# Two edits at the start of a tuned state-space kernel: the source of the warm-up matmuls, and the size of the transposing loads of B

## The chip, the cores and the metric

The kernel runs on one core of one Trainium2 chip. The metric is the device time of one execution in microseconds (us), lower is better. A time is the span of the profile plus about 1.8 us (the profiled run of the kernel before took 247.9 us with a span of 246.1). All times compared here are of runs at a granted TensorE clock of 0.997 to 1.0 of full speed. Each group of experiments below ran on another chip.

## The reference, cut to what matters

The output is a gated mix of two branches over x (2048 tokens of 1024 features, bf16): a diagonal complex state-space model, and a branch that adds a gated MLP to the 8 best-scored tokens.

```python
x = A_x
g = sigmoid((x * gate_w).sum(-1, keepdims=True))
# a: state-space model
Lam_bar = exp(dt * Lam)                              # complex, diagonal
B_bar = ((Lam_bar - 1.0) / Lam)[:, None] * (B_re + 1j * B_im)
Bu = einsum("bld,pd->blp", x + 0j, B_bar)            # needs B_re and B_im transposed
h = Lam_bar * h + Bu[:, t, :]                        # for every t
a = 2.0 * einsum("blp,dp->bld", hseq, C_re + 1j * C_im).real + x * Dskip
# b: x + (silu(x_sel @ w_gate) * (x_sel @ w_up)) @ w_down, for the 8 tokens of highest x @ w_r
return g * a + (1 - g) * b
```

What matters here is the product with B. B_re and B_im are 1024 x 1024 matrices that come to the chip transposed, in eight chunks of 128 rows each (c = 0 to 7); the matmuls use chunk after chunk, re before im.

## The kernel before

The loads stand on the queue of SyncE, in this order (cut):

```python
def load_B(pl, c0, c1):                               # pl 0: re, 1: im; rows c0*128 to c1*128
    nc.sync.dma_start_transpose(BT[pl][:, :, c0 * P:c1 * P], Bsrc[pl][c0 * P:c1 * P, :])

load_B(0, 0, 1)
...
load_xT(1)
load_B(1, 0, 1)
for c0, c1 in ((1, 2), (2, 3), (3, 4), (4, 6), (6, 8)):
    for pl in range(2):
        load_B(pl, c0, c1)
load_X(1)                                             # second block of x: two transposing loads
for pl in range(2):
    load_C(pl, 0)
...
load_X(2)                                             # third block
load_C(0, 512)
load_X(3)                                             # last block
load_C(1, 512)
```

TensorE is kept busy with matmuls on a tile of zeros until the first tokens are there:

```python
wt0 = small.tile([P, LC], BF16, name="wt0", tag="wt")
nc.vector.memset(wt0[:], 0.0)
...
def warm(n):
    for _ in range(n):
        nc.tensor.matmul(wps[:], lhsT=wt0[:, 0:P], rhs=wt0[:], start=True, stop=True)

warm(14)
```

Then come the products with B, eight matmuls of 512 columns for the re part of a chunk and eight for the im part (the first chunk apart).

```python
def s1u(m, ct, pl, k0, k1):                           # block m, chunk ct, re or im
    ...
    for dc in range(KD):
        nc.tensor.matmul(o, lhsT=BT[pl][:, dc, ct * P:(ct + 1) * P], rhs=X[m][:, dc, k0 * LC:k1 * LC], ...)

def gate_rows():
    zr = ps_m.tile([P, 2 * LC], F32, name="zr", tag="m")
    for dc in range(KD):
        for m in range(4):                            # the last block too
            nc.tensor.matmul(zr[32 * m:32 * m + 32, :], lhsT=rg[:, dc, :], rhs=X[m][:, dc, :], ...)
```

Of the kernel before, what the change touches and what calls it, by code (L numbers as in the profile page):

```python
# [11 lines left out]
BF16 = mybir.dt.bfloat16  # L12
# [4 lines left out]
P = 128  # L17
LC = 256
# [6 lines left out]
def kernel(  # L25
# [19 lines left out]
    nc = tc.nc  # L45
# [3 lines left out]
    NCT = NP_ // P  # L49
# [16 lines left out]
    small = ctx.enter_context(tc.tile_pool(name="small", bufs=1))  # L66
# [12 lines left out]
    def load_B(pl, c0, c1):  # L79
        nc.sync.dma_start_transpose(BT[pl][:, :, c0 * P:c1 * P], Bsrc[pl][c0 * P:c1 * P, :])  # L80
# [18 lines left out]
    new_X(0)  # L99
    load_xT(1)  # L100
    load_B(1, 0, 1)
    for c0, c1 in ((1, 2), (2, 3), (3, 4), (4, 6), (6, 8)):
        for pl in range(2):
            load_B(pl, c0, c1)
    load_X(1)
# [19 lines left out]

    stpool = ctx.enter_context(tc.tile_pool(name="stpool", bufs=2))

    wt0 = small.tile([P, LC], BF16, name="wt0", tag="wt")
    nc.vector.memset(wt0[:], 0.0)
    Dbc = const.tile([P, D], BF16, name="Dbc")  # L130
    halfpi = small.tile([P, 1], F32, name="halfpi")
    nc.vector.memset(halfpi[:], math.pi / 2)
# [15 lines left out]
    wps = ps_m.tile([P, LC], F32, name="wps", tag="m")  # L148

    def warm(n):  # L150
        for _ in range(n):
            nc.tensor.matmul(wps[:], lhsT=wt0[:, 0:P], rhs=wt0[:], start=True, stop=True)

    warm(14)
    vec = small.tile([P, 3, NCT], F32, name="vec")
    for tl in range(BPC):
        xq = ps_s2.tile([P, KD, P], BF16, name="xq", tag="zps")
# [2 lines left out]
        for h, copy in enumerate((nc.vector.tensor_copy, nc.scalar.copy)):  # L160
            hs = slice(h * KD // 2, (h + 1) * KD // 2)
            copy(out=X[0][:, hs, tl * P:(tl + 1) * P], in_=xq[:, hs, :])
    warm(2)
    va_ps = ps_m.tile([P, 3, NCT], BF16, name="va_ps", tag="m")
    for i in range(3):
# [230 lines left out]

    tab_neg(0)
    warm(1)
    s1u(0, 0, 0, 0, 1)
    warm(2)  # L400
# [547 lines left out]
```

## Time and profile before

| | kernel before |
|---|---|
| three timed runs | 247.28, 247.49, 247.5 us |
| the run that was profiled | 247.9 us (span 246.1) |
| TensorE busy | 240.6 of 246.1 us |
| the wait for B_im, chunk 4 | 0.89 us |
| the tail: start of VectorE's last instruction to the end of the span | 3.18 us |

In the lines of the profile PE is TensorE, PEld its loading of weights, DVE VectorE, ACT ScalarE, POOL GpSimd and SPq the queue of SyncE; L485 is line 485 of the kernel. First, the page's list of DMA queues (queue, kind: packets, MB, share of 16 engines):

```profile
q8 instruction: 11, 0.18, 0.3%
q14 instruction: 6, 0.05, 0.1%
```

The engines' own instructions come in by DMA too. 17 packets and 0.3% look like nothing, but each of the eleven is 16 KB in one packet.

### The profile page before, as it was taken

What the parts mean: (1) busy time and instruction counts of PE and PEld (TensorE: products, weight loads), DVE (VectorE), ACT (ScalarE), POOL (GpSimd) and SP (SyncE); (2) the same over time, 40 slices, a digit from 0 to 9 for tenths busy, and PEclk for the clock granted to TensorE, in tenths of its full rate; (3) what the DMA queues carried; (4) which work ended last, traced back from release to release, by engine and by line L of the source; (5) the groups of instructions that cost most, each with busy time, mean ns of one, the idle gap of its engine ahead of it and who ended that gap; (6) DMA issues with size and microseconds to landing.
All of it is one profiled execution on the core that took longest, in us unless ns stands there. A gap on an engine that the chain in (4) does not pass through costs nothing.

```text
span 246.1 us, 3533 instructions
## 1 busy us (share of the span) xinstructions
PE 240.6 (98%) x1381; PEld 112.2 (46%) x1381; DVE 226.2 (92%) x230; ACT 119.3 (48%) x206; POOL 26.8 (11%) x47
## 2 busy tenths in 40 slices
PE   8998999999999999999999999999999999999994
PEld 5443444444444444444444444444444444446453
DVE  1799999999999999999999999999999999999932
ACT  3699973333462572223355462235267445456421
POOL 4000000000000301620002040100100211110210
PEclk9999999999999999999999999999999999999999
DMA  7899999999760450666257979778599999962052
GB/s 195 194 149 226 230 244 273 202 239 284 236 181 0 106 153 0 134 125 224 77 188 218 351 226 338 237 224 314 184 390 286 363 306 296 89 142 37 3 133 82
DMA packets 65313, 48.48 MB, mean 197 GB/s; under 512 B 50560, under 2 KB 52224, under 8 KB 65296
## 3 DMA queue, kind: packets, MB, share of 16 engines
q1 hardware_dynamic: 59968, 37.20, 58.1%
q0 software_dynamic: 3264, 7.38, 14.3%
q10 hardware_dynamic: 2064, 3.68, 4.1%
q8 instruction: 11, 0.18, 0.3%
q14 instruction: 6, 0.05, 0.1%
HBM read 27.55 MB, written 8.40 MB: 146 GB/s over the span
## 4 chain that ended last, share of the span: by engine, by line
PE 89%; SPq 7%; DMA 2%; issue 0%; DVE 0%
PE zps L767 42%; PE vps L271 39%; SPq L80 6%; PE zps L783 3%; PE pgu L659 3%; DMA BT<-in_A_B_im_dram 2%; PE y L671 1%; SPq L92 1%; PE zr L485 1%; DVE ot L788 0%; SPq L77 0%; PE xselT_ps L572 0%; PE zs_ps L588 0%; PE zt L492 0%; PE fl_ps L535 0%
## 5 line engine op out<-in xcount | busy, mean ns | idle before, releaser
L271 PE MATMUL vps<-X,BT 128*128 128x512 bf16 (+1 forms) x520 | 112.6, 376 | 1.2 <-DMA BT<-in_A_B_im_dram 0.9
L767 PE MATMUL zps<-CT,H 128*128 128x512 bf16 x480 | 105.0, 379 | 0.0
L271 PEld LDWEIGHTS <-BT 128*128 128x128 bf16 x520 | 50.1, 98 | 61.7 <-DMA BT<-in_A_B_im_dram 1.7
L767 PEld LDWEIGHTS <-H 128*128 128x128 bf16 x480 | 46.5, 98 | 56.6 <-issue 1.3
L278 ACT CAST V<-vps 128x512 bf16<-128x512 f32 x64 | 34.3, 588 | 58.6 <-PE vps L271 58.6
L308 DVE TENSOR_TENSOR_SCAN U<-d,U 128x2048 bf16<-128x2048 f32 (+2 forms) x22 | 62.0, 2860 | 0.6
L772 ACT ACTIVATE ot<-zps,gcol 128x512 bf16<-128x512 f32 x30 | 20.6, 686 | 46.3 <-PE zps L767 46.3
L741 ACT CAST zps<-xd 128x512 f32<-128x512 bf16 (+1 forms) x29 | 16.6, 576 | 3.6 <-ACT xt L728 3.3
L297 DVE TENSOR_TENSOR U<-V,T2tab 128x4096 bf16<-128x4096 bf16 (+2 forms) x11 | 16.6, 1511 | 0.7 <-ACT V L278 0.2
L298 DVE TENSOR_TENSOR V<-V,nTi 128x4096 bf16<-128x4096 bf16 (+2 forms) x11 | 16.7, 1516 | 0.5
L299 DVE TENSOR_TENSOR U<-U,V 128x4096 bf16<-128x4096 bf16 (+2 forms) x11 | 16.7, 1516 | 0.4
L793 POOL DMA_DIRECT2D out_dram<-ot x14 | 12.9, 923 | 32.5 <-ACT ot L772 30.4
L333 DVE TENSOR_TENSOR U<-U,S2tab 128x4096 bf16<-128x4096 bf16 x7 | 16.0, 2292 | 0.2
L335 DVE TENSOR_TENSOR H<-H,U 128x4096 bf16<-128x4096 bf16 x7 | 16.0, 2292 | 0.2
L728 ACT ACTIVATE xt<-xt,omgcol 128x1024 bf16<-128x1024 bf16 x14 | 16.0, 1144 | 0.0
L331 DVE TENSOR_TENSOR H<-U,Ctab 128x4096 bf16<-128x4096 bf16 x7 | 16.0, 2284 | 0.0
L705 POOL DMA_DIRECT2D xt<-in_A_x_dram x12 | 7.1, 594 | 80.9 <-DMA out_dram<-xt 42.9
L366 DVE TENSOR_TENSOR_SCAN U<-D,U 128x1024 bf16<-128x1024 f32 x4 | 8.9, 2279 | 0.1
L723 DVE TENSOR_TENSOR xd<-xt,Dbc 128x1024 bf16<-128x1024 bf16 x14 | 9.0, 683 | 0.0
L659 PE MATMUL pgu<-wgu,xsel 128*32 128x448 bf16 x128 | 7.2, 355 | 0.0
L783 PE MATMUL zps<-CT,H 128*128 128x256 bf16 (+1 forms) x48 | 7.1, 308 | 0.0
L718 POOL DMA_DIRECT2D out_dram<-xt x2 | 1.5, 752 | 49.2 <-DVE xt L717 49.2
(152 smaller groups left out, 127.6 us busy)
## 6 DMA issues: line engine op xcount, KB each, us to landing
wgu<-in_B_w_gate_dram SPq DMA_DIRECT2D x16, 448.0 KB, 3.5
wgu<-in_B_w_up_dram SPq DMA_DIRECT2D x16, 448.0 KB, 6.1
out_dram<-ot POOLq DMA_DIRECT2D x14, 256.0 KB, 6.0
wdb<-in_B_w_down_dram SPq DMA_DIRECT2D x7, 512.0 KB, 10.6
xt<-in_A_x_dram POOLq DMA_DIRECT2D x12, 256.0 KB, 4.3
out_dram<-xt ACTq DMA_DIRECT2D x12, 256.0 KB, 5.2
wd<-in_B_w_down_dram SPq DMA_DIRECT2D x5, 512.0 KB, 7.8
xt<-in_A_x_dram SPq DMA_DIRECT2D x4, 256.0 KB, 4.1
```

The costliest lines, as they stand in the source:

```text
L271: nc.tensor.matmul(o, lhsT=BT[pl][:, dc, ct * P:(ct + 1) * P], rhs=X[m][:, dc, k0 * LC:k1 * LC], start=(dc == 0), stop=(dc == KD - 1))
L278: nc.scalar.copy(out=V[k][:, :, ct, :], in_=vp[m, ct][:, :, kk, :])
L297: nc.vector.tensor_tensor(out=u, in0=v, in1=T2tab[:, :, c0:c1, :], op=ALU.mult)
L298: nc.vector.tensor_tensor(out=v, in0=v, in1=bc(nTi, c0, c1), op=ALU.mult)
L299: nc.vector.tensor_tensor(out=u, in0=u, in1=V[k][:, ::-1, c0:c1, :], op=ALU.add)
L308: nc.vector.tensor_tensor_scan(out=fl, data0=d0[:, c0:c1, :].rearrange("p c t -> p (c t)"), data1=fl, initial=0.0, op0=ALU.mult, op1=ALU.add)
L331: nc.vector.tensor_tensor(out=h, in0=g, in1=bc(Ctab, c0, c1), op=ALU.mult)
L333: nc.vector.tensor_tensor(out=g, in0=g, in1=S2tab[:, :, c0:c1, :], op=ALU.mult)
L335: nc.vector.tensor_tensor(out=h, in0=h, in1=G[k][:, ::-1, c0:c1, :], op=ALU.add)
L741: nc.scalar.copy(out=z[:], in_=xd[b][:, d_:d_ + w])
L767: nc.tensor.matmul(zps[:], lhsT=H[k][:, pl, ct, tl * P:(tl + 1) * P], rhs=CT[pl][:, ct, dsl], start=(fresh and ct == 0 and pl == 0), stop= ...
L772: nc.scalar.activation(out=ots[b][:, dsl], in_=zps[:], func=ACT.Copy, scale=gcol[:, b:b + 1])
```

## The change

The intent: let the warm-up begin without waiting for a memset on VectorE, and let TensorE have chunk 4 of B_im without waiting for chunk 5, which came in the same 256-row load.

```diff
-    for c0, c1 in ((1, 2), (2, 3), (3, 4), (4, 6), (6, 8)):
+    for c0, c1 in ((c, c + 1) for c in range(1, NCT)):
         for pl in range(2):
             load_B(pl, c0, c1)
...
-    wt0 = small.tile([P, LC], BF16, name="wt0", tag="wt")
-    nc.vector.memset(wt0[:], 0.0)
+    wt0 = nc.const_aps.tensor(1.0, [P, LC], BF16)
...
-            nc.tensor.matmul(wps[:], lhsT=wt0[:, 0:P], rhs=wt0[:], start=True, stop=True)
-    warm(14)
+            nc.tensor.matmul(wps[:], lhsT=wt0[:, 0:P], rhs=wt0, start=True, stop=True)
+    warm(16)
```

It adds four DMA instructions and two matmuls, and takes one memset away.

## The prediction

> **What bounds the kernel now.** I read the page first (busy shares, slices, the chain that ended last), then the waits of the TensorE, then the timeline of the first 30 us on the queue of SyncE, and last the timelines of TensorE, ScalarE and VectorE for the slack behind the start.
>
> The page, shares of the span:
> ```profile
> span 246.1 us, 3533 instructions
> PE 240.6 (98%) x1381; PEld 112.2 (46%) x1381; DVE 226.2 (92%) x230; ACT 119.3 (48%) x206; POOL 26.8 (11%) x47
> ```
> PE is busy for 240.6 of 246.1 us, so all that any change of waits can give is in the other 5.5 us, and 2 to 3 us of those are the tail after the last matmul. The view of waits, limited to PE and to the first 40 us, has all the idle time there is:
> ```profile
> PE wps L152 <- DVE halfpi L132: 1.1, 1, 1.1
> PE vps L271 <- DMA BT<-in_A_B_im_dram: 0.9, 2, 0.7
> PE vps L271 <- DMA X<-in_A_x_dram: 0.2, 1, 0.2
> ```
> The reader is to see that the kernel waits for B in just two places, and that the larger is 0.7 us. (The 1.1 us at the start is the time before the first warm-up matmul.) In the chain that ended last, the same wait is the hinge between the loads and the 219 us of unbroken matmuls; the columns are start, length and what ran:
> ```profile
> 14.68 3.56 SPq L80
> 18.24 0.04 issue
> 18.29 5.27 DMA BT<-in_A_B_im_dram
> 23.56 0.05 issue
> 23.61 36.43 PE vps L271 x168
> ```
> So one load of B_im, issued at 18.29, lands at 23.56 and releases PE at 23.61. The timeline says which. On the queue of SyncE, in order of time:
> ```profile
> 11.97 1.31 SPq L80 DMA_TRANSPOSE BT<-in_A_B_re_dram  x1
> 13.33 1.31 SPq L80 DMA_TRANSPOSE BT<-in_A_B_im_dram  x1
> 14.68 3.56 SPq L80 DMA_TRANSPOSE BT<-in_A_B_re_dram  x1
> 18.29 2.42 SPq L80 DMA_TRANSPOSE BT<-in_A_B_im_dram  x1
> 20.75 2.18 SPq L80 DMA_TRANSPOSE BT<-in_A_B_re_dram  x1
> 22.98 2.42 SPq L80 DMA_TRANSPOSE BT<-in_A_B_im_dram  x1
> 25.44 4.40 SPq L92 DMA_TRANSPOSE X<-in_A_x_dram  x2
> ```
> The first two are the last 128-row loads (c=3); the next four are the 256-row loads (c=4..5, then c=6..7, re and im in turn). The one that lands late is B_im rows 4..5: PE wants only its half 4, but gets it when both are there. The size of the loss: the first matmul of re c=4 starts at 20.99 (timeline of PE in short windows), eight matmuls at 36.43/168 = 0.2168 us are 1.73 us, so im c=4 could start at 22.72 and starts at 23.61: 0.89 us lost. (The view of waits says 0.7 as it counts from the modelled end of the matmul before.) Re c=4 itself cost nothing: the matmuls before it start at 20.12, 20.34, 20.55, 20.77, and the next slot is 20.99.
>
> **What the Trainium skill says.** "TensorE: Matmul & The Clock Gate", Part 1 (the HAM clock gate): the array starts at 1.2 GHz and goes to 2.4 after about 3.4 us of activity, in a window that runs free, so that the point varies; cold matmuls start N/1.2 GHz apart. The trace agrees in kind: 14 warm-up matmuls of 256 columns fill 1.07 to 4.13, which is 13 at 256/1.2 = 0.213 us and one short one, so the clock changed near 3.85, some 2.8 us after the first. The same part gives 215.7 ns between warm matmuls of 512 columns; here it is 216.8. "DMA: Bandwidth & Descriptors", Rules for kernel authors, advises 1 MiB or more per DMA and to merge small ones, which speaks against the cut into 256 KB pieces; the same page, Latency and other measured facts, has 261 GB/s for a DMA transpose with a non-contiguous middle dimension. In the trace the 128-row loads went out at 256 KiB per 1.35 us, 194 GB/s; the 256-row ones at 512 KiB per 2.2 to 2.4 us, 218 to 238 GB/s, the first of them at 147. So larger is somewhat faster per byte here too, and no run has yet shown 128-row loads in that place.
>
> **The change part by part.**
> (1) The memset of the warm-up tile (0.17 us on VectorE, from 0.84) goes, and the warm-up reads a constant that the preamble has already written (GpSimd, 0.31 to 0.41). The warm-up waited for VectorE until 1.07. The other engines start at 0.74 to 0.75, so I take PE's start as about 0.80: 0.27 us earlier. Two more matmuls are 2 x 0.213 = 0.43 us if cold, 2 x 0.11 = 0.22 if warm. The last warm-up starts at 0.80 + 15 x 0.213 = 4.0 if all are cold, and leaves PE at about 4.1 to 4.2. Before, the transposes of x began at 4.11 when x0r had landed. So they move by 0 to +0.1 us. Behind them stand three waits for transfers: PE waits at 5.93 for the first B_re (0.24 us on the weight loader), at 7.44 for X (0.24) and at 8.65 for the first B_im (0.18). None of those transfers moves, so a shift of 0.1 ends there. Worth on the path: 0.0.
> (2) Four 256-row loads become eight of 128 rows in the order re 4, im 4, re 5, im 5, re 6 and so on. Issued from 14.68 at 1.35 us each: re 4 at 14.68, im 4 at 16.03, re 5 at 17.4, im 5 at 18.7, im 7 at 24.1 to 25.4. The view of B's tile has 3.4/4.7/5.3 us as least, median and most from issue to landing. With 4.7: im 4 lands at 20.7, wanted at 22.72; re 5 at 22.1, wanted at 20.99 + 16 x 0.2168 = 24.46; im 5 at 23.4, wanted at 26.2. If the odd 0.95 us that the first 256-row issue took above the second-longest kind (3.56 against 2.60 for the X load at 2.57) strikes again, im 4 goes out at 17.0 and lands at 21.7: still 1.0 us early. So the wait at 23.61 goes whole: -0.89 us.
> (3) What comes after. SyncE ends the B loads at 14.68 + 8 x 1.35 = 25.5 against 25.40 before, or 26.4 with the odd stall. X of the second block then lands by 32.4 to 33.6 (second issue plus 5.0, the median of X), and PE wants it at 23.61 - 0.89 + 56 x 0.2168 = 34.86. No wait.
> (4) Does the gain reach the end? ScalarE must empty PSUM: it waited for PE by 0.18, 0.72, 0.49 and 1.43 us in its next evictions, and the one that did not wait, c=5 (29.11 to 30.18), frees the buffer that PE wants for c=7 at 32.28, or 31.39 after. VectorE is 92% busy and moves less than PE: its one wait there is 0.24 us at 36.52, so it gains at most that. Then PE's lead over its inputs shrinks by 0.65 us or more, at most 0.89. The nearest places, VectorE's end against PE's use:
> ```profile
> 73.04 2.29 DVE L335 TENSOR_TENSOR H<-H,U 128x4096 bf16<-128x4096 bf16 x1
> 204.75 2.29 DVE L335 TENSOR_TENSOR H<-H,U 128x4096 bf16<-128x4096 bf16 x1
> 231.50 0.69 DVE L380 TENSOR_TENSOR H<-H,U 128x1024 bf16<-128x1024 bf16 x1
> 235.80 7.11 PE L783 MATMUL zps<-CT,H 128*128 128x512 bf16 x48
> ```
> H of chunk 1 is done at 75.3 and used at 65.50 + 64 x 0.217 = 79.4 (4.1 us free); chunk 6 at 207.0, used near 211.8 (4.8); the first half of the last one at about 232.2, used at 235.80 (3.6). The update rows land at 237.4 and are added by 238.7, where the last add for which they are needed stands at 241.92. All over 0.89. So the sum is 0.0 - 0.89 + 0.0 = -0.89 us, carried by PE to the end: 247.49 - 0.89 = 246.60 us, -0.36%.
>
> **The rivals.**
> (a) The 128-row loads are slower and the wait only moves. For it: per byte they went out 10 to 20% slower than the larger ones, and the skill's advice. Against: im 4 has 1 to 2 us to spare. If it holds, im 4 lands at 22.72 or later, or X of the second block becomes the wait, and the gain is 0 to 0.5: 247.0 to 247.5.
> (b) VectorE takes PE's place as the bound. For it: 92% busy, without idle time of note from 14 to 234 us. Against: the slack of 3.6 us and more above. If it held, nothing of the gain would be left: 247.4.
> (c) The clock. The warm-up ends about where it did, but its two ends move in the free-running window. If the clock came a window later, the matmuls from 5.93 to 10.6 (16 of 256 columns and 8 of 512, 8192 columns, 3.5 us warm) would run cold, and with the waits between them I put 1 to 2 us on it: 247.6 to 248.6. Against: activity begins earlier and has no new gap. If it came earlier, nothing is gained, as x0r and B set the pace there.
> (d) All is hidden or the start gains too: an earlier first matmul brings 0.2 us more, 246.4. Against: three waits for transfers behind it.
>
> **Range and chances.** I give the sum 70%, (a) 15%, (c) 5%, the rest to (b) and (d). The three timed runs before span 0.22 us, which I take as noise of 0.15 to either side, and the sum's own doubt is 0.1 or 0.2. So 246.6, with 246.2 to 247.1 for 8 in 10. A change of 2% is 4.9 us; the idle time of PE before 23.61 is less than that in all. Faster by over 2%: 0.005; slower by over 2%: 0.01, for a clock that stays low or a load that stalls; within 2%: 0.985.
>
> **What would show it.** Right: PE's waits list no wait for B_im over 0.2 us, and the matmuls run unbroken from about 10.6; the eight B issues after c=3 last about 1.3 us each, the first perhaps 2.3; the chain's long run of matmuls begins at about 10.6 and its end is near 242.1; the span is about 245.2. The first warm-up starts near 0.80 and the transposes of x still near 4.1 to 4.2. Wrong: a wait for B or X on PE at 21 to 35 us (rival a), PE waiting for H or zps (b), 0.2 us spacing of 256-column matmuls after 5.9 (c), or a later start of B's first loads on SyncE.

## More of the kernel before

The end. VectorE's last instruction in its timeline, and SyncE's wait on line 943, where the body of the kernel is closed, in the view of waits of its queue (us in total, times, longest):

```profile
242.95 0.48 DVE L788 SCALAR_TENSOR_TENSOR ot<-zps,gcol,xt 128x256 bf16<-128x256 f32 x1 [0.21 <-PE zps L783]
```

```profile
SPq L943 <- DMA out_dram<-ot: 0.8, 2, 0.5
```

The span ends at 246.14, so 3.18 us pass after the last arithmetic begins (the tail; from unrounded times); they hold the last store and the closing waits of SyncE.

Second, TensorE's timeline near 60 us (start, length, engine, line, operation, tiles, shapes, count), where the gate reads the last block of x:

```profile
59.97 1.91 PE L485 MATMUL zr<-X,rg 128*32 128x512 bf16 x32
```

## The result, and the profile after

| | before | after |
|---|---|---|
| timed runs, us | 247.19, 247.28, 247.49, 247.5, 247.58, 247.58 | 247.46, 247.55, 247.55, 247.76, 248.01, 249.09 |
| median, us | 247.5 | 247.66 |
| profiled run, us (span) | 247.9 (246.1) | 247.46 (245.7) |

The ratio is 1.0019, with a 95% interval of 0.9995 to 1.0042: the same time within 2%. This ratio is the mean time of one kernel's fast runs over that of the other's. In the experiments below the ratios leave out the first run of each kernel (of the kernel tested, the profiled one), so they are not quite the ratios of the means given beside them. The predicted 246.6 did not come, nor any time in the range of 246.2 to 247.1.

The page, and the view of waits of TensorE in the first 40 us:

```profile
span 245.7 us, 3541 instructions
PE 241.1 (98%) x1383; PEld 112.7 (46%) x1383; DVE 225.8 (92%) x229; ACT 119.2 (49%) x206; POOL 26.9 (11%) x47
```
```profile
PE wps L151 <- PEq L931: 0.8, 1, 0.8
```

So the wait for B_im is gone, and so is the one for X. The timeline on SyncE's queue shows why (start, length of the issue, line, tile, count):

```profile
14.68 2.38 SPq L80 DMA_TRANSPOSE BT<-in_A_B_re_dram  x1
17.10 1.31 SPq L80 DMA_TRANSPOSE BT<-in_A_B_im_dram  x1
18.45 1.31 SPq L80 DMA_TRANSPOSE BT<-in_A_B_re_dram  x1
...
26.56 4.73 SPq L92 DMA_TRANSPOSE X<-in_A_x_dram  x2
...
52.49 4.13 SPq L92 DMA_TRANSPOSE X<-in_A_x_dram  x2
```

Chunk 4 of B_im went out at 17.10 and landed at 20.90, where the prediction had 20.7 to 21.7, and TensorE wanted it at about 22.6. The chain that ended last (start, length, what ran) now leaves the loads before 9 us:

```profile
8.49 1.90 PE vps L270 x8
...
10.52 48.45 PE vps L270 x224
58.98 2.22 PE zr L484 x32
61.19 3.56 PE vps L270 x16
```

From 10.52 to 58.98 TensorE does not stop. But the gate takes 2.22 us in this chain against 1.84 before (1.91 in the timeline above). The timeline of the weight loads has the reason:

```profile
59.29 1.41 PEld L484 LDWEIGHTS <-rg 128*32 128x32 bf16 x29 [0.29 <-DMA X<-in_A_x_dram]
```

The last block of x, issued at 52.49 to 56.62, landed at 59.25; before it had landed at 55.45. And the end, in the same two views as before:

```profile
242.26 0.48 DVE L787 SCALAR_TENSOR_TENSOR ot<-zps,gcol,xt 128x256 bf16<-128x256 f32 x1 [0.21 <-PE zps L782]
```
```profile
SPq L942 <- DMA out_dram<-ot: 1.1, 1, 1.1
```

VectorE's last instruction begins 0.69 us earlier than before (242.26 against 242.95), but the span ends only 0.45 us earlier (245.69 against 246.14): the tail is 3.42 us instead of 3.18.

The two traces balance as follows. The unbroken run of matmuls began 0.16 us earlier (the first of c=1 at 10.46 instead of 10.62), from there to the gate it took 0.90 less (the wait for chunk 4), the gate 0.38 more, the tail 0.24 more: -0.44, against -0.45 between the two spans. So in this pair of traces the predicted 0.89 us are there, and about two thirds of them were given back in places where the prediction had nothing. But the pair of traces says faster by 0.45 us and the timed runs say slower by 0.16 at the median. The kernel before, then, must usually run without most of the loss that its trace showed. That was to be tested.

### The profile page after: what moved, and what is told of

Read it like the earlier page. It is cut to its first block, busy times and chain, and to the rows that moved or that the text cites. A ratio compares the mean times of both kernels' runs of the same rounds, so it can differ in the third digit from the quotient of the medians.

```text
span 245.7 us, 3541 instructions
## 1 busy us (share of the span) xinstructions
PE 241.1 (98%) x1383; PEld 112.7 (46%) x1383; DVE 225.8 (92%) x229; ACT 119.2 (49%) x206; POOL 26.9 (11%) x47
## 4 chain that ended last, share of the span: by engine, by line
PE 95%; SPq 2%; DMA 1%; DVE 0%; issue 0%
PE vps L270 45%; PE zps L766 42%; PE zps L782 3%; PE pgu L658 3%; DMA BT<-in_A_B_im_dram 1%; PE y L670 1%; SPq L92 1%; PE zr L484 1%; SPq L80 1%; DVE ot L787 0%; SPq L77 0%; PE xselT_ps L571 0%; PE zs_ps L587 0%; PE zt L491 0%; PE vb_ps L435 0%
```

## The experiments

Theories at the start. (i) The wait is a draw: it differs from run to run, the trace before came from a long run, and its mean is well under 0.89. (ii) It is there in every run, and the gain is given back later, at the gate and in the tail. (iii) A delay at chunk 4 is hidden behind some slack, so that taking it away changes nothing. (iv) The new warm-up costs what the loads gain.

Means and medians are of six runs of the kernel, and of eleven of the kernel before in the same rounds. The mean and median of the kernel before were 247.88 and 247.8 in the first group (four kernels), 247.65 and 247.45 in the second (four), 248.34 and 248.12 in the third (four) and 248.39 and 248.27 in the fourth (three).

### First group: the same again, and each part alone

**The kernel before, unchanged.** No edit.

> The kernel before, unchanged, as a control. Theory 1 (the gain at the c=4 wait is real and is given back later, at the gate matmuls, where the profile after shows 0.3 us of waiting for X): its trace again loses 0.8 to 0.9 us at c=4 and nothing at the gate. Theory 2 (the profile of before was an odd draw, it was taken in a run of 247.9 us where the others have 247.2 to 247.6, and the usual wait at c=4 is smaller): the trace loses under 0.5 us at c=4 and its run is 247.2 to 247.6. Time 247.4 for both, ratio 1.000 within 0.001.

Measured: mean 247.77, median 247.57, ratio 0.9987 (0.996 to 1.0014), six runs from 247.27 to 248.76. Its trace is of the 248.76 run. The waits of TensorE, and the queue of SyncE:

```profile
PE vps L271 <- DMA BT<-in_A_B_im_dram: 1.4, 2, 1.0
...
PE vps L271 <- DMA BT<-in_A_B_re_dram: 0.5, 1, 0.5
```
```profile
14.57 4.23 SPq L80 DMA_TRANSPOSE BT<-in_A_B_re_dram  x1
18.84 2.56 SPq L80 DMA_TRANSPOSE BT<-in_A_B_im_dram  x1
```

The same code, another size: the first 256-row issue took 4.23 us, not 3.56, and chunk 4 of B_im landed at 24.41, not 23.56. Now TensorE waits for chunk 4 of B_re too, 1.83 us in all where the trace before lost 0.90, which fits neither of the two sizes expected. The wait is no constant, which is the first half of theory (i). The six runs are also a measure of the noise: the same kernel differs from itself by 0.11 us on the mean, and by 0.32 in the runs of the ratio.

**The kernel after, unchanged.** No edit.

> The changed kernel, unchanged, as a control of its spread: six runs had 247.46 to 249.09, against 0.4 us of spread before. Theory 1: the trace has no wait at c=4 and one of 0.3 us or more on X at the gate matmuls, and the slow runs are those where X comes later still. Theory 2: no wait at the gate in most runs, 247.4. Theory 3 (the warm-up change costs something, for example granted clock, as some of its runs list 0.999): a clock of 0.999 with the slower runs. Time 247.5 to 247.8.

Measured: mean 247.73, median 247.76, ratio 0.9995 (0.9968 to 1.0023). No wait at chunk 4 in its trace; chunk 4 of B_im landed at 20.67. The last block of x landed at 58.02, and here the gate did not wait: what it lost in the first trace is a draw as well. The tail was 3.43, again a quarter of a microsecond longer than before.

**The loads alone**, with the old warm-up:

```diff
-    for c0, c1 in ((1, 2), (2, 3), (3, 4), (4, 6), (6, 8)):
+    for c0, c1 in ((c, c + 1) for c in range(1, NCT)):
```

> Only the eight 128-row loads, with the old warm-up. Theory 1: no wait at c=4, a wait for X at the gate of 0.3 us or more, net 247.2 to 247.7. Theory 2: 247.3, as there is little to win. Theory 3: 246.6 to 246.9, since what costs is left out.

Measured: mean 247.67, median 247.72, ratio 0.9994 (0.9968 to 1.0021). Chunk 4 landed at 20.18; no wait there and, against what theory (ii) expected, none at the gate; tail 3.44.

**The warm-up alone**, with the old loads:

```diff
-    wt0 = small.tile([P, LC], BF16, name="wt0", tag="wt")
-    nc.vector.memset(wt0[:], 0.0)
+    wt0 = nc.const_aps.tensor(1.0, [P, LC], BF16)
...
-    warm(14)
+    warm(16)
```

> Only the warm-up change, with the 256-row loads. Theory 1 and theory 2: as before within 0.1 us (247.4), the c=4 wait as in the control. Theory 3: 247.8 or more, and the spread of the changed kernel comes with it.

Measured: mean 247.58, median 247.57, ratio 0.999 (0.9962 to 1.0018), tail 3.18. In its trace the 256-row loads are the old ones, and there is no wait at chunk 4:

```profile
14.81 3.13 SPq L80 DMA_TRANSPOSE BT<-in_A_B_re_dram  x1
```

The issue took 3.13 us, chunks 4 and 5 of B_im landed at 22.57, and TensorE wanted them at about 22.8 (48 + 8 matmuls after 10.70). So a 256-row load can be in time. Neither part moves the time outside the interval, and theory (iv) has nothing for it. The long tail goes with the loads, not with the warm-up.

### Second group: what the wait is worth, and what a microsecond of it is worth

**No wait by other data.** In the kernel before, chunks 4 to 7 of the first block use chunks 0 to 3 of B, which have long landed. The result is wrong on purpose (though the comparison's tolerance let it pass).

```diff
         for dc in range(KD):
-            nc.tensor.matmul(o, lhsT=BT[pl][:, dc, ct * P:(ct + 1) * P], ...)
+            cb = ct - 4 if m == 0 and ct >= 4 else ct
+            nc.tensor.matmul(o, lhsT=BT[pl][:, dc, cb * P:(cb + 1) * P], ...)
```

> The kernel before, but in the first block column chunks 4 to 7 of B are replaced by chunks 0 to 3, which landed long ago, so no wait for B can arise after c=3 (wrong result on purpose). All loads stay as they are. It measures what the c=4 wait is worth in the timed runs. Theory 1 (0.89 us in every run): 0.8 to 0.9 us under the kernel before. Theory 2 (the wait differs from run to run, the first profile caught a long one): 0.3 to 0.6 us under the mean of before, and the slow tail of before (248.5 and more) is gone. Theory 4 (something else than PE's waits sets the end, so that time on PE is not worth time at the end): under 0.1 us.

Measured: mean 247.38, median 247.42, ratio 0.9992 (0.9966 to 1.0018), six runs from 247.20 to 247.54. Against the kernel before in the same rounds (246.89 to 248.97) the mean falls by 0.26 us and the median by 0.03; what vanishes are the long runs. In its own trace the loads of chunk 4 landed at 22.44, so that this run would have lost nothing had it waited. This sizes the wait: about a quarter of a microsecond on the mean, next to nothing in the median run. The interval, some 0.6 us to either side, is wider than that, and the unchanged kernel differed from itself by as much, so 0.26 is a reading and not a proof. That six runs have no long one, where 3 of 11 are over 248, can also be chance. And it is one chip: the kernel before was slower on two others (medians of 248.1 and 248.3), where this was not run.

**One more load ahead of chunk 4, kernel before.** It goes into a part of the C tile that is filled later.

```diff
             load_B(pl, c0, c1)
+        if c1 == 4:
+            nc.sync.dma_start_transpose(CT[1][:, :, 512:640], Bsrc[1][0:128, :])
```

> The kernel before with one more 128-row transposing load (1.35 us on the queue, into a part of C that is loaded again later) ahead of the loads of c=4. If the c=4 wait is on the path in a usual run, the whole 1.35 us shows at the end: 1.2 to 1.4 us over before (theories 1 and 2). If a usual run has slack there of s us, 1.35 - s. Theory 4: nothing shows.

Measured: mean 248.81, median 248.72, ratio 1.0052 (1.0022 to 1.0082): 1.16 us more on the mean, 1.27 on the median, for an issue of 1.31 us and a gap of 0.04. All six runs are over 248.2. Its trace:

```profile
PE vps L273 <- DMA BT<-in_A_B_im_dram: 0.5, 1, 0.5
```

Chunk 4 of B_im landed at 23.96. Theory (iii) falls: a delay ahead of chunk 4 comes out at the end nearly whole. It also says that the loads have close to no slack in the kernel before: most of its runs stand just at the edge of waiting.

**The same load in the kernel after.** The same edit.

> The changed kernel with the same extra load. If im 4 has the slack of 1 to 2 us that the prediction worked out, PE waits at c=4 by 0 to 0.3 us only, but X of the last block comes 1.35 us later and the gate matmuls wait 1 to 1.7 us in theory 1 (time +1 us or more), 0.3 to 1 us in theory 2. If the 128-row loads leave no slack at c=4: +1.2 us with the wait at c=4.

Measured: mean 248.14, median 248.09, ratio 1.0022 (0.9996 to 1.0049), 0.67 us under the other kernel with the extra load. The single-chunk loads do give the slack that the prediction claimed: nothing waits at chunk 4. What waits is the second block of x, which landed at 35.43, and not the last block at the gate, as was expected:

```profile
35.52 24.33 PE L272 MATMUL vps<-X,BT 128*128 128x512 bf16 x110 [0.56 <-PE vps L272]
```

(The view names a matmul as the releaser; the landing at 35.43 and the start at 35.52 say that it was the transfer.) The next input in the queue is late in turn: the prediction's rival (a), with the load doubled to bring it out.

**The last block of x ahead of C, kernel after.**

```diff
     load_X(2)
-    load_C(0, 512)
     load_X(3)
+    load_C(0, 512)
     load_C(1, 512)
```

> The changed kernel with X of the last block loaded ahead of the second half of C, so that the gate matmuls at 59 us cannot wait for it. Theory 1 (gain given back at the gate): 0.3 us or more under the changed kernel (247.4 or less against 247.7), smaller spread. Theory 2 (the wait at the gate is an odd draw as well): within 0.2 us of the changed kernel. The trace has no wait for X at the gate under either.

Measured: mean 247.36, median 247.31, ratio 0.9986 (0.996 to 1.0013), 0.3 us under the kernel before on the mean. The last block's first half landed at 53.7, and the gate does not wait. It fits a loss at the gate in some runs of the kernel after, but the interval takes in no change.

### Third group: the tail, the gate, a better order, and what draws the wait

**Four tiny loads more, kernel after.** If the tail depends on how many DMAs there are, four 128-byte loads will change it.

```diff
+    scr = small.tile([1, 4, 64], BF16, name="scr")
...
     def zero_last():
+        for i in range(4):
+            nc.sync.dma_start(scr[:, i, :], x2d[i:i + 1, 0:64])
```

> The changed kernel with four tiny loads (128 bytes each, unused) added on SyncE's queue in the middle. The traces so far have 3.14 to 3.20 us from the start of the last VectorE instruction to the end of the span in the kernels with the 256-row loads, and 3.44 to 3.46 in those with eight 128-row loads. Theory 5 (the closing waits: eight semaphores are dealt in turn to the DMAs and waited for one by one in a fixed order at the end, some 60 ns each; four more loads move the last store's semaphore from the fifth place to the first, so that the rest is waited for after it): with eight more DMAs than before the place is the old one, and the tail is 3.15 to 3.20 again, time 0.25 us under the changed kernel. If the tail belongs to the 128-row loads in another way, it stays at 3.45.

Measured: mean 248.11, median 248.26, ratio 0.9985 (0.9953 to 1.0018). The tail went back to 3.18 us, and SyncE's last wait reads `DMA out_dram<-ot: 0.8, 2, 0.5`, as in the kernel before. The records of SyncE after its last store show the mechanism. They are a row of equal waits, each of 28 ns, and all are done about 60 ns apart except where a store is still under way:

| kernel | the wait for the last store ends ... us before the end | waits still to come | tail, us |
|---|---|---|---|
| before | 1.092 | 3 | 3.18 |
| after | 1.339 | 7 | 3.42 |
| after, unchanged again | 1.339 | 7 | 3.43 |
| after, four tiny loads more | 1.094 | 3 | 3.18 |
| before with two more loads (below) | 0.973 | 1 | 3.06 |

The kernel ends by waiting once for each of a fixed row of semaphores. The records of DMAs name eight of them in turn, so four more or fewer DMAs anywhere in the kernel move the last store from one place in the row to another. Before, the last store stood late in the row; after, it is first, all others are checked behind it, and 4 x 0.06 us come on top. With eight more DMAs it is back where it was. The two kernels with one extra load, traced before this was looked for, fit as well: their last store stands one place later in the row than without it, and their tails are 3.12 and 3.37.

What undid the gain in this trace was the gate:

```profile
60.54 1.90 PE L485 MATMUL zr<-X,rg 128*32 128x512 bf16 x29 [1.07 <-DMA X<-in_A_x_dram]
```

The last block of x landed at 60.50, and from the product before the gate to the one after it TensorE lost 1.46 us, the largest loss so far (the view counts 1.07 of it as idle). The tiny loads come far behind, so up to here this is the kernel after: another draw of the same race.

**The kernel after, a third time.** No edit.

> The changed kernel a third time, beside the two above on the same chip: 247.5 to 247.8 on average, no wait at c=4, X of the second block landing at 33.3 to 34.6 against the 34.7 at which PE wants it, tail 3.45.

Measured: mean 248.18, median 248.14, ratio 0.9994 (0.9963 to 1.0025). No wait at chunk 4; the last block of x landed at 59.60, and the gate lost 0.15 us. Tail 3.43.

**The fetch of instructions, moved.** In every trace but that of this experiment one packet of 16,384 bytes comes on the instruction queue at 14.7 to 17.1 us. While it is under way some of the 256-byte packets of the transposing queue, 18 ns at the median, take far longer, the longest of each trace 1.27 to 2.49 us, and in all 17 traces the issue that runs at that time is a long one:

```text
trace                    packet at   took   longest packet of B   the long issue   chunk 4 of B_im landed
before                   16.72       0.95   1.43                  3.56             23.56
before, unchanged again  16.08       2.15   2.49                  4.23             24.41
warm-up alone            16.42       0.95   1.36                  3.13             22.57
(us; from the trace's records of single DMA packets)
```

If that packet is the cause, it should follow the number of instructions that TensorE has run. So 28 warm-up matmuls of 128 columns take the place of 14 of 256, with the same columns in all:

```diff
-    warm(14)
+    for _ in range(28):
+        nc.tensor.matmul(wps[:, 0:P], lhsT=wt0[:, 0:P], rhs=wt0[:, 0:P], start=True, stop=True)
```

> Every trace has one 16 KB packet of the instruction queue at 14.7 to 16.7 us, and the transposing load that is being issued or in flight then takes 0.5 to 1.6 us longer. Theory 6 (TensorE's instruction fetch holds up the loads of B): the 14 warm-up matmuls of 256 columns are replaced by 28 of 128, the same time with 28 instructions more, which is about 3 us of later work; the packet comes some 3 us earlier, at 13 to 14 us, and the long issue moves from the 11th transposing load to the 9th or 10th. If the stall belongs to the first 256-row load, it stays at the 11th and the packet may be anywhere.

Measured: one run of 247.3 (one look, state unknown, so its time is not used). The packet came at 13.62, and on SyncE's queue:

```profile
13.42 2.30 SPq L80 DMA_TRANSPOSE BT<-in_A_B_im_dram  x1
15.76 2.69 SPq L80 DMA_TRANSPOSE BT<-in_A_B_re_dram  x1
```

The lengthening moved one load up, to a 128-row load that takes 1.31 us in every other trace, and the first 256-row issue took 2.69, close to its kind. A limit in the loads' own queue (always the tenth load, say) would have stayed where it was; in other traces it is at the tenth or, as in the next kernel, at the eleventh. So the stall belongs to the fetch. A second packet, of 8,192 bytes, came at 22 to 25 us wherever the old warm-up was traced, and near 30 to 31 with the new one; in the trace before (22.09, 0.66 us) it fell on the load that was wanted.

**Only what the wait needs.** The kernel before with chunks 4 and 5 alone in loads of their own, the old warm-up, and the last block of x ahead of C:

```diff
-    for c0, c1 in ((1, 2), (2, 3), (3, 4), (4, 6), (6, 8)):
+    for c0, c1 in ((1, 2), (2, 3), (3, 4), (4, 5), (5, 6), (6, 8)):
...
     load_X(2)
-    load_C(0, 512)
     load_X(3)
+    load_C(0, 512)
     load_C(1, 512)
```

> The version that the runs point to: the kernel before with its old warm-up, only c=4 and c=5 of B in 128-row loads (c=6 to 7 stays a 256-row load), and X of the last block ahead of the second half of C. im 4 should land at about 20.5 against 22.4 to 24.4 with the 256-row load, X of the second block at about 33.0 to 33.5, the tail 3.05 to 3.15 (the last store's semaphore is the seventh of eight). No wait on PE after c=0. 247.2 us on average and no run over 247.8, against 247.4 to 247.7 and runs up to 249 before.

Measured: mean 247.32, median 247.29, ratio 0.9956 (0.9927 to 0.9985). TensorE waits for no transfer after c=0 in its trace; chunk 4 of B_im landed at 20.27, the second block of x at 32.73, the last at about 50.6 for its first half; the tail is 3.06. It is the first interval of a kernel with less waiting that leaves out 1.

Its trace has a loss of another kind, too short for the view of waits: between chunk 1 and the gate TensorE took 0.37 us more than in the traces without a wait. The chain that ended last shows it:

```profile
4.27 1.90 PE xq L159 x16
...
9.69 1.24 DVE tf L212
...
10.95 1.06 ACT nTi L223
12.01 1.04 ACT T2tab L224
...
13.49 0.97 ACT V L278 x2
...
14.51 5.45 PE vps L271 x24
```

The 16 transposes of x ran at the low clock, 107 ns apart, where the trace before had them 56 ns apart (1.07 us in all); by the traces' records of the granted clock it rose at 6.69 us here and at 3.88 there. The tables that ScalarE makes come later with them, and so do its evictions (V), which free the memory of the products (PSUM) for chunk 2. Five traces lost 0.07 to 0.38 us in this way before chunk 4 (those with 1.61 us or more for the transposes), two with the new warm-up and three with the old one; in each TensorE goes on about 0.05 us after an eviction has ended.

### Fourth group: is that better kernel real, and which of its parts counts

**The same kernel again, on another chip.** No further edit.

> The same kernel as the one with two 128-row loads and X first, in a second job. If its gain is real: again about 247.3 us on average with no run over 247.8, 0.3 to 1.0 us under the kernel before, depending on how many long runs that one has in this job; tail 3.05 to 3.10.

Measured: mean 247.29, median 247.26, ratio 0.9954 (0.9923 to 0.9985), six runs from 247.00 to 247.57. It holds.

**Without the new order of x and C**: only the first of the two edits above.

> The kernel before with c=4 and c=5 of B in 128-row loads and nothing else. If two more loads do not delay X of the last block as eight do: X issued by 53.5 and landed by 56, no wait at the gate, 247.2 to 247.4 on average, as with X first. If they do: X lands at 58 or later and the time is 247.5 or more. Tail 3.05 to 3.10 in both.

Measured: mean 247.80, median 247.66, ratio 0.9969 (0.9935 to 1.0003). The trace is of a 248.31 run, whose loss lies at the front, in code that no kernel here changed: the first B_im landed at 9.95 instead of 8.6, and TensorE waited 1.1 us for it. The last block of x landed at 56.87, in time for the gate, but the time is above the 247.2 to 247.4 that were expected for that case.

**With the new warm-up**: the kernel after, with

```diff
-    for c0, c1 in ((c, c + 1) for c in range(1, NCT)):
+    for c0, c1 in ((1, 2), (2, 3), (3, 4), (4, 5), (5, 6), (6, 8)):
```

> The same two 128-row loads with the new warm-up. If the new warm-up is worth nothing either way: within 0.15 us of the run with the old one, the first matmul after c=0 at 10.5 to 11.0 in both. If it takes part in the lateness of X: X lands 2 us or more later than with the old warm-up.

Measured: mean 248.15, median 248.12, ratio 0.9978 (0.9945 to 1.0011). The trace is of its longest run, 249.22, and the largest wait of TensorE is

```profile
PE zr L484 <- DMA X<-in_A_x_dram: 1.6, 1, 1.6
```

The last block of x landed at 61.37. This is the gate's race again, with two loads fewer than the kernel after. In all traces the gate waited only in kernels with the new warm-up and the old order of x and C (in three of the four traces of the kernel after and its variant with tiny loads, and in this one; not with the warm-up alone, and not with the extra load). In those traces two 8 KB instruction packets come together at 30 to 31 us, and the load of C behind them takes 6.8 to 7.8 us to issue instead of 4.1 to 4.4. But the better kernel showed such a load once too (6.85 us), with the old warm-up. The last block landed 4.5 us later here than with the old warm-up and the same loads, more than the 2 us that were set beforehand as the mark of the warm-up's part; but these are single traces, and this one is of the longest run. So it is shown that this race exists and what losing it costs (2.02 us here); whether the new warm-up tilts it was not settled. Between these kernels with two single-chunk pairs, the intervals overlap, and the kernel before with the new order of x and C alone was not run.

**All 17 traces on one balance.** From the product after the gate to the start of VectorE's last instruction they all take 181.14 us, whatever the kernel. From the first product of c=1 to the last one before the gate they take 48.14 us where nothing waits, and over the gate 2.15. So their spans differ in four places alone: the start of c=1 (10.46 to 11.96 us), the losses between there and the gate (0 to 1.83), those at the gate (0 to 2.02), and the tail (3.06 to 3.44). A loss before or at the gate comes out at the end whole, and nothing is lost elsewhere. With the earliest start and no loss the kernel before would have a span of 10.46 + 48.14 + 2.15 + 181.14 + 3.18 = 245.07 us. Its shortest run had 245.1 (246.89), so some of its runs lose next to nothing, which is the other half of theory (i). But on the chips of the third and fourth group its median spans, 246.3 and 246.5, stand 1.2 and 1.4 us above this; none of those runs was traced, and how that is shared among the start, the wait and the gate stays open.

## Why the prediction was wrong

**The bound.** Right: TensorE bounds the kernel, and a delay of TensorE before 25 us reaches the end almost one to one (1.16 to 1.27 us for 1.35; in the traces whole).

**Step (1), the warm-up, 0.0 us.** Right. It begins at 0.78 where 0.80 was said. The first matmul of c=1 begins at 10.50 to 10.85 with the old warm-up (but for the trace with the late B_im) and at 10.46 to 11.03 with the new one.

**Step (2), the wait for chunk 4, "-0.89".** The mechanism was right: chunk 4 of B_im lands at 20.2 to 21.7 in every kernel that loads it alone (22.55 behind the extra load), and no such kernel waits for it. The size is the step that failed. The 0.89 us were one draw. The wait depends on where the instruction packets fall and how long they take: it was 0.89 in one trace of the kernel before, 1.83 with chunk 4 of B_re in the other, nothing in the trace with the warm-up alone. Taking the wait away brought 0.26 us on the mean and 0.03 on the median, on one chip and with an interval that takes in no change. The prediction called the lengthened issue an "odd 0.95 us" that might strike again, and asked only whether the new loads could bear it; it did not ask how often the old ones had to. The hint was in hand: the profiled run took 247.9, the timed ones 247.28 to 247.5. What a trace shows is to be subtracted from the run that was traced. 247.9 - 0.89 is 247.0, with nothing else wrong, and not 246.6.

**Step (3), "No wait".** It looked at the second block of x, and for that it was right (landed at 34.13, later than the predicted 32.4 to 33.6, wanted at about 34.7; the prediction's own figures, 25.5 plus 2.3 to the second issue plus 5.0, give 32.8 and not 32.4 for the lower end). It did not look at the block that has the same queue and another use: the gate reads the last block at 59 us, and in the kernel after it lands between 58.0 and 60.5. That cost 0 to 1.46 us in the traces, 0.38 in the first one.

**Step (4), the gain reaches the end.** VectorE had room, as said, and rival (b) showed in no trace. Rival (c), the clock, showed in a small form, in kernels with either warm-up: where the clock rose 2.8 to 2.9 us later than in the trace before, the loss was 0.22 and 0.37 us, through ScalarE, and not the 1 to 2 that the prediction put on it. But the step took the tail for fixed (at 2 to 3 us after the last matmul, where its own line gives 246.1 - 242.9 = 3.2), and the tail grew by 0.25 us, since four more DMAs moved the last store to the front of the row of closing waits.

**The sum.** As far as these readings go, -0.26 for the wait and +0.25 for the tail cancel on the mean, and the gate adds something that differs from run to run. The kernel after stood at +0.47, -0.15 and -0.16 us against the kernel before by the means of the three groups in which it ran unchanged. All agree with about nothing. "Noise of 0.15 to either side" from three runs was also too small: eleven runs of the kernel before spread over 2.0 to 2.2 us in each group, and with the wait taken away six runs spread over 0.34.

**What would show it.** The prediction's list named a chain that begins at about 10.6, a first issue of "perhaps 2.3" (it was 2.38) and no wait for B_im. All that came true, and the span of 245.2 and the time did not. The marks were of the wait's going, not of what its going was worth.

The kernel that splits chunks 4 and 5 only and brings the last block of x forward is better than both: 247.3 us on two chips, 0.45% under the kernel before. Three places are put right in its traces (the wait, the gate, and the tail at 3.06); what each of them is worth was not separated. None of its twelve runs is over 247.8, against 16 of the 22 of the kernel before in the same rounds; its mean is near that of the kernel that cannot wait for B at all (247.38, on another chip). How large the ratio is depends on how often the kernel before has its long runs, and that differed between the groups.

## What to carry to other kernels

Before you price a wait from one trace, compare the time of the traced run with the timed runs, and trace the unchanged kernel a second time: a wait on a transfer that lands near the moment of its use is a draw, and only its mean over runs can be gained. When loads in one queue are cut or delayed, follow every later load of that queue to its own first use, not just the next one. The number of DMAs and of instructions has costs of its own here, in the closing waits and in the fetches that stall a stream of small packets, so cut only the loads that are waited for.

## What the Trainium skill lacked or had wrong

- "DMA: Bandwidth & Descriptors", Queues, rings and completion order, says that each DMA engine takes turns between rows a packet at a time, and names refill among the uses of row 14. It lacks what this costs a stream of small packets: one instruction packet of 16,384 bytes (0.95 us, up to 2.15) held some 256-byte packets of a transposing load for up to 1.27 to 2.49 us instead of 18 ns, and lengthened an issue on SyncE from 1.31 us to 1.8 to 3.2. In these traces instruction packets came on queue 8 as well as on queue 14, as the profile numbers them.
- No page found has the closing waits: SyncE goes through a row of semaphores at about 60 ns each, and where the last store stands in it moved the end by 0.12 to 0.25 us (tails of 3.06, 3.18 and 3.42 us) with the number of DMAs in the kernel.
- The same DMA page, Rules for kernel authors, advises large DMAs. For bytes per time the runs agree (1.31 us for 128 rows, 1.9 to 2.5 for 256 where nothing stalled). For the time of the kernel the best version had two pairs of small loads where data was wanted at once, and large ones elsewhere (ratio 0.9954 and 0.9956).
- The page "TensorE: Matmul & The Clock Gate", Part 1, has the window that runs free, so that the clock changes at another point in every run, and gives the change as around 4 us into the activity, within 0.5 us to either side. The runs agree that it varies, but by more: the records put the rise 2.7 to 6.0 us after the first warm-up matmul, the 16 transposes of x behind it took 1.07 to 1.91 us, and the late ones cost up to 0.38 us.
